# Chunk-selected attention and an ELU MLP on one core: relu written to SBUF, longer rows for the first loads, a new instruction order

## The chip, the cores and the metric

The kernel runs on one core of one Trainium2 chip. The metric is device time in microseconds. The engines are PE (TensorE), DVE (VectorE), ACT (ScalarE), POOL (GpSimd) and SP (SyncE, which here only issues DMAs).

## The reference

Attention of 4 batches, 8 heads, 768 tokens and 64 dimensions per head, in which each query sees 6 of 24 key chunks of 32 tokens, followed by an MLP over 3072 tokens.

```python
k_min, k_max = min and max of k over each chunk of 32 keys
ub = sum over d of max(q * k_min, q * k_max)        # causal, per query and chunk
top_chunks = the 6 chunks of largest ub
scores = q @ k.T / 8, masked to those chunks and to earlier keys
x = softmax(scores) @ v                             # to (3072, 512)
h = x @ w_in                                        # (3072, 2048)
g = where(h > 0, h, exp(min(h, 0)) - 1)
out = g @ w_out                                     # (3072, 512), float32
```

## The kernel before

The work is cut into pairs of heads (a unit `u` is a batch's pair; 16 in all) and halves of 384 tokens. For a pair, K and Q are loaded from HBM and turned so that the head dimension lies on partitions; chunk minima and maxima are taken; a matmul gives the bounds `ub`; DVE finds the sixth largest (`quad_sel`, L551) and compares against it (L614, both inputs in SBUF); POOL puts the result into extra rows of Q (L631), where it acts as a mask in the score matmul (L672). ACT takes the exp (L699), POOL cuts the causal diagonal (L718), PE multiplies with V (L731), DVE normalises (L747), PE transposes (L756) and ACT stores `xT` (L759). When a batch's four pairs have their `xT`, the MLP of that batch and half can run (`mlp`, L763).

Batch 0 has its own preparation (`first_prep`, L443). K and Q of a pair and half come as 96 partitions with 4 tokens each, a row of 1 KB per head, into the big tiles `gT`, which the MLP uses later, and into `stage` and `kt`; the function `home` says where. `turn` (L492) transposes them on PE by 8 matmuls of 96 columns with a float32 identity (L498). ACT copies K and Q out (L508, L526, L531), DVE reduces K (L514, L521), and POOL casts Q (L548) and V (L539). The other batches use `pair_prep` (L386), with DVE transposes (L409, L427), reductions (L413) and POOL casts (L548, L440).

In the MLP, a chunk `fc` of 128 hidden units takes four matmuls into a PSUM bank (L781), then the ELU, then, when four chunks are there, down matmuls (L838). The ELU of a chunk has three forms:

- batches 0 to 2, chunk listed in `BOTH`: ACT exp to `e` in SBUF (L791), ACT relu in place in PSUM (L796), DVE `min(e - 1, relu)` from SBUF and PSUM (L799)
- batches 0 to 2, other chunks: ACT exp, DVE `t = max(e - 1, h)` (L820), DVE `min(max(h, 0), t)` (L825), each with one input in PSUM
- batch 3 (`FAST`): ACT exp, DVE L809 and L814, two chunks at a time

A list in `BOTH` has the chunks of one half; each batch has two halves.

The order of instructions is worked out in Python before anything is emitted. Every operation is added to a `Plan` with an engine, an estimated duration, its data, the buffers that it takes and frees, and a rank (`prio`). `Plan.order` (L119) goes through time on these estimates: on each engine, of the operations that could start first, the one of lowest rank goes next. Buffers come from small pools: four single PSUM banks shared by the MLP's chunks, its outputs, the turns and the transposes; two double banks for scores; three each of `e`, `t` and `gT`. Operations marked `port=True`, and all of POOL, are planned so that a marked DVE operation and a POOL operation do not overlap. The engines then run their instructions strictly in that order. DMAs of K, Q, V and the output are issued by SP, two of the first Q loads by ACT, the weights by POOL.

```python
add("DVE", dve(step * HALF), pr,
    lambda e=e, t=t, view=view: nc.vector.scalar_tensor_tensor(
        out=tiles[t][:, 0:step], in0=tiles[e][:, 0:step], scalar=1.0, in1=view(),
        op0=AOT.subtract, op1=AOT.max),
    reads=[(e, 0), bh[0]], writes=[t], alloc=[t], free=[e])
```

Here `view()` is the PSUM bank `bh`; it is freed by the second DVE operation.

Of the kernel before, what the change touches and what calls it, by code (L numbers as in the profile page):

```python
# [10 lines left out]
AOT = mybir.AluOpType  # L11
# [6 lines left out]
S = 768  # L18
# [20 lines left out]
BOTH = {0: (0, 1, 4, 5, 8, 9, 12, 13), 1: (0, 1, 2, 3, 4, 5, 8, 9, 10, 11, 12, 13), 2: (1, 5, 9, 13), 3: ()}  # L39
# [13 lines left out]
RATES = (232.0, 232.0, -1.4, 0.75)  # L53
MERGE = (False, False, False, True)

# [8 lines left out]
class Plan:  # L64
# [53 lines left out]

    def order(self):  # L119
# [77 lines left out]
def kernel(  # L197
# [188 lines left out]
    def pair_prep(u):  # L386
# [52 lines left out]
        add("POOL", 0.13 + 0.00096 * S, pr + 1.0,  # L439
# [3 lines left out]
    def first_prep(u, hf):  # L443
# [18 lines left out]
        def home(i):  # L462


            if i < 12:
                if i % 6 == 0:
                    STAGED[i // 6], = new("gT")
                h = STAGED[i // 6]
                return h, [h] if i % 6 == 0 else [], [h] if i % 6 == 5 else [], lambda: tiles[h][:, i % 6]
            h, = new("stage" if i < 15 else "kt")  # L470
            return h, [h], [h], lambda: tiles[h][:, 0:512]
# [13 lines left out]
        (hk, ak, fk, at_k), (hq, aq, fq, at_q) = home(i0), home(i0 + 1)  # L485
        fetch(0.5, 197.0, RATES[0], pl, load(at_k, kw, nc.sync), [(hk, i0)], alloc=ak)
        fetch(0.5, 197.0, RATES[0], pl + 0.1, load(at_q, qw, nc.scalar if early else nc.sync), [(hq, i0 + 1)],
# [4 lines left out]
        def turn(bb, at):  # L492
            def f():
                p_ = ps(bb, [P, HALF], F32)
                for j in range(4):
                    for hd in range(2):
                        x0 = 256 * hd + 64 * j
                        nc.tensor.matmul(p_[64 * hd:64 * hd + 64, 96 * j:96 * j + 96], lhsT=at()[0:96, x0:x0 + 64],  # L498
                                         rhs=ident_f[0:96, 0:96], start=True, stop=True)
            return f  # L500

        def tok(x):

            return x.rearrange("q (j p) -> q p j", j=4)
        add("PE", TURN, pr, turn(bk, at_k), reads=[(hk, i0), "ident"], writes=[bk[0]], alloc=bk, free=fk)
        for hd in range(2):
            add("ACT", act(HALF), pr,
                lambda hd=hd: nc.scalar.activation(  # L508
                    out=tiles[kb][0:64, hd, a:b].rearrange("q (p j) -> q p j", j=4),
                    in_=tok(ps(bk, None, None)[64 * hd:64 * hd + 64, :]), func=AF.Copy),  # L510
                reads=[bk[0]], writes=[(kb, hf, hd), (bk[0], "turn")], alloc=[] if hf or hd else [kb])
        for x, op in ((0, AOT.min), (1, AOT.max)):
# [3 lines left out]
                    in_=ps(bk, None, None).rearrange("q (j c w) -> q c j w", j=4, w=CHUNK // 4),  # L516
# [9 lines left out]
            lambda: nc.scalar.activation(out=tiles[qt][:, a:b].rearrange("q (p j) -> q p j", j=4),  # L526
# [5 lines left out]
                out=tiles[qa][:, lo - SEL0:b - SEL0].rearrange("q (p j) -> q p j", j=4),  # L532
                in_=tok(ps(bq, None, None))[:, (lo - a) // 4:], func=AF.Relu),
# [4 lines left out]
        add("POOL", 0.13 + 0.00096 * HALF, pr + 1.0,  # L538
# [6 lines left out]
    def cast(pr, w, what, **kw):  # L545
# [3 lines left out]
        add("POOL", 0.13 + 0.00096 * w, pr, f, **kw)  # L549
# [213 lines left out]
    def mlp(b, hf):  # L763
        tail = b == B - 1
        if True:
# [3 lines left out]
            for fc in range(0, NFC, step):  # L769
# [24 lines left out]
                if both:  # L794
                    add("ACT", act(step * HALF), pr,
                        lambda view=view: nc.scalar.activation(out=view(), in_=view(), func=AF.Relu),  # L796
                        reads=[bh[0]], writes=[bh[0]])
                    add("DVE", dve(step * HALF), pr,
                        lambda e=e, view=view, fc=fc, gt=gt: nc.vector.scalar_tensor_tensor(  # L799
                            out=tiles[gt][:, fc:fc + step, :], in0=tiles[e][:, 0:step], scalar=1.0, in1=view(),  # L800
                            op0=AOT.subtract, op1=AOT.min),
                        reads=[(e, 0), bh[0]], writes=[(gt, fc + i) for i in range(step)],
                        alloc=[gt] if fc == 0 else [], free=bh + [e])
                    continue
                t, = new("t")
                fast = FAST[b]
                if fast:
                    add("DVE", 0.32 + 0.00021 * step * HALF, pr,
                        lambda e=e, t=t: nc.vector.tensor_scalar(  # L809
                            out=tiles[t][:, 0:step], in0=tiles[e][:, 0:step], scalar1=1.0, scalar2=1.0,  # L810
                            op0=AOT.min, op1=AOT.subtract),
                        reads=[(e, 0)], writes=[t], alloc=[t], free=[e], port=True)
                    add("DVE", dve(step * HALF), pr,
                        lambda t=t, view=view, fc=fc, gt=gt: nc.vector.tensor_tensor(  # L814
                            out=tiles[gt][:, fc:fc + step, :], in0=tiles[t][:, 0:step], in1=view(), op=AOT.max),
                        reads=[t, bh[0]], writes=[(gt, fc + i) for i in range(step)],
                        alloc=[gt] if fc == 0 else [], free=bh + [t])
                    continue
# [118 lines left out]
```

## Time and profile before

| | |
|---|---|
| runs | 280.21, 280.38, 285.49 us; median 280.38 |
| span of the profiled execution (first to last instruction) | 278.4 us, some 2.0 under the median of the runs |
| time of the profiled execution itself | not given beside its span |
| granted TensorE clock | 1.000 |
| DVE, ACT, POOL busy | 204.2, 201.4, 128.0 us |

In the profile, busy time is the union of an engine's instructions. An instruction's recorded duration overlaps a little with that of the next one on its engine, so distances between starts are shorter than durations. Groups of instructions are shown as line, engine, operation, out<-in, shape and count, then busy us and the mean ns of one, then the engine's idle time before them and what ended it.

### The profile page before, as it was taken

The numbers are of one execution on the slowest core, as the hardware profiler recorded it, in microseconds if no ns is written. First come the engines' busy times: TensorE is split into PE (matmuls) and PEld (weight loads), VectorE is DVE, ScalarE is ACT, GpSimd is POOL, SyncE is SP. The second block draws the span as 40 slices with busy tenths as digits, with TensorE's granted clock in tenths as the row PEclk, the third lists the DMA queues.
The fourth block names the chain that finished last, engine by engine and source line by source line (L and its number), as shares of the span: only waits on it lengthen the run. The fifth ranks groups of instructions, "written<-read, shape, count | busy, mean of one in ns | idle before, by whom it ended". The sixth has DMA issues, their size and how long they took to land.

```text
span 278.4 us, 7242 instructions
## 1 busy us (share of the span) xinstructions
PE 266.7 (96%) x2732; PEld 164.0 (59%) x2732; DVE 204.2 (73%) x546; ACT 201.4 (72%) x381; POOL 128.0 (46%) x235
## 2 busy tenths in 40 slices
PE   7989899989999999999999999999999999999994
PEld 7968566644565556655665656565565556555541
DVE  6876965799999989999989588657856434767610
ACT  2879899946699697999899958685868564544311
POOL 5668863356797797966965625102320201000000
PEclk9999999999999999999999999999999999999999
DMA  7999999988998599999497101101101111101122
GB/s 187 232 211 188 197 203 207 146 131 163 189 171 156 73 143 201 165 163 170 87 164 114 38 2 38 40 0 40 39 4 38 40 39 40 38 0 40 38 75 75
DMA packets 111330, 29.82 MB, mean 107 GB/s; under 512 B 101056, under 2 KB 108224, under 8 KB 111296
## 3 DMA queue, kind: packets, MB, share of 16 engines
q1 hardware_dynamic: 106656, 24.78, 48.4%
q0 software_dynamic: 4224, 4.19, 9.2%
q8 instruction: 21, 0.34, 0.6%
q10 hardware_dynamic: 416, 0.39, 0.5%
q14 instruction: 13, 0.11, 0.1%
HBM read 27.26 MB, written 6.29 MB: 121 GB/s over the span
## 4 chain that ended last, share of the span: by engine, by line
PE 68%; ACT 15%; DVE 6%; DMA 4%; issue 3%; SPq 1%; POOL 0%; ACTq 0%; DVEq 0%
PE psM L838 20%; PE psH L781 15%; PE psS L781 7%; PE psMT L838 7%; PE psS L672 7%; ACT pt L699 7%; PE psO L731 5%; ACT e L791 3%; PE psS L580 3%; DMA gT<-in_v_dram 2%; DMA gT<-in_k_dram 2%; ACT psH L796 1%; ACT xT L759 1%; DVE gT L799 1%; PE psT L756 1%
## 5 line engine op out<-in xcount | busy, mean ns | idle before, releaser
L699 ACT ACTIVATE pt<-psS 128x768 bf16<-128x768 f32 (+1 forms) x120 | 91.5, 799 | 4.1 <-PE psS L672 2.6
L781 PE MATMUL psH<-xT,w_in_sb 128*128 128x384 bf16 x384 | 75.2, 325 | 1.6 <-ACT xT L759 0.9
L838 PE MATMUL psM<-w_out_sb,gT 128*128 128x512 bf16 x288 | 72.5, 379 | 0.4 <-DVE gT L825 0.2
L781 PEld LDWEIGHTS <-w_in_sb 128*128 128x128 bf16 x512 | 47.6, 97 | 34.8 <-issue 4.0
L791 ACT ACTIVATE e<-psH 128x384 f32<-128x384 f32 x96 | 48.3, 519 | 22.4 <-PE psH L781 21.9
L838 PEld LDWEIGHTS <-gT 128*128 128x128 bf16 x384 | 36.2, 98 | 35.0 <-DVE gT L825 0.6
L718 POOL TENSOR_SCALAR_AFFINE_SELECT pt<-pt 128x256 bf16<-128x256 bf16 (+1 forms) x56 | 29.0, 519 | 56.7 <-ACT pt L699 55.7
L672 PE MATMUL psS<-rhs,lhs 88*128 88x384 bf16 (+4 forms) x304 | 51.5, 283 | 1.6 <-ACT pt L699 0.9
L672 PEld LDWEIGHTS <-lhs 88*128 88x128 bf16 x304 | 27.8, 97 | 15.8 <-issue 1.5
L631 POOL COPY rhs<-selt 24x192 bf16<-24x192 bf16 (+2 forms) x56 | 25.5, 456 | 21.9 <-DVE selt L620 18.6
L799 DVE SCALAR_TENSOR_TENSOR gT<-e,psH 128x384 bf16<-128x384 f32 x48 | 25.6, 539 | 13.3 <-ACT psH L796 13.2
L731 PEld LDWEIGHTS <-pt 128*128 128x128 bf16 x672 | 27.8, 98 | 11.3 <-issue 3.8
L548 POOL CAST rhs<-qt 64x768 bf16<-64x768 f32 (+1 forms) x40 | 28.5, 711 | 12.3 <-ACT qt L526 6.1
L820 DVE SCALAR_TENSOR_TENSOR t<-e,psH 128x384 bf16<-128x384 f32 x48 | 25.9, 543 | 9.6 <-ACT e L791 9.2
L731 PE MATMUL psO<-vext,pt 128*128 128x65 bf16 x672 | 30.2, 194 | 1.7 <-DVE gT L799 1.1
L791 ACT ACTIVATE e<-psS 128x768 f32<-128x768 f32 x16 | 13.0, 810 | 19.0 <-PE psS L781 19.0
L825 DVE SCALAR_TENSOR_TENSOR gT<-psH,t 128x384 bf16<-128x384 f32 x48 | 25.9, 543 | 0.8
L796 ACT ACTIVATE psH<-psH 128x384 f32<-128x384 f32 x48 | 25.1, 528 | 0.0
L781 PE MATMUL psS<-xT,w_in_sb 128*128 128x384 bf16 x128 | 23.2, 326 | 0.0
L548 POOL CAST lhs<-kt 64x768 bf16<-64x768 f32 x24 | 19.6, 819 | 6.8 <-DVE kt L409 3.7
L838 PE MATMUL psMT<-w_out_sb,gT 128*128 128x512 bf16 x96 | 22.5, 379 | 0.0
L759 ACT ACTIVATE xT<-psT 128x384 bf16<-128x384 bf16 x32 | 16.5, 515 | 4.5 <-PE psT L756 4.4
(66 smaller groups left out, 293.4 us busy)
## 6 DMA issues: line engine op xcount, KB each, us to landing
out_dram<-osb SPq DMA_DIRECT2D x24, 256.0 KB, 2.0
vd<-in_v_dram SPq DMA_DIRECT2D x12, 384.0 KB, 5.2
stage<-in_k_dram SPq DMA_DIRECT2D x48, 96.0 KB, 3.4
stage<-in_q_dram SPq DMA_DIRECT2D x48, 96.0 KB, 3.6
w_in_sb<-in_moe_w_in_dram POOLq DMA_DIRECT2D x4, 512.0 KB, 11.5
w_out_sb<-in_moe_w_out_dram POOLq DMA_DIRECT2D x4, 512.0 KB, 8.8
gT<-in_v_dram SPq DMA_DIRECT2D x16, 96.0 KB, 4.3
gT<-in_k_dram SPq DMA_DIRECT2D x6, 192.0 KB, 5.5
```

The source lines that it names most:

```text
L548: nc.gpsimd.tensor_copy(out=o, in_=i)
L672: nc.tensor.matmul(p_s[:, hd, pc:pc + w], lhsT=tiles[pt_["kb"]][0:64 + NCH, hd, 128 * kb:128 * kb + 128], rhs=tiles[pt_["qb"]][0:64 + NCH, ...
L699: lambda bs=bs, pt=pt, wtot=wtot, lo=lo, at=at: nc.scalar.activation(out=tiles[pt][:, :, lo:lo + wtot], in_=tiles[bs[0]][:, :, at:at + wto ...
L718: nc.gpsimd.affine_select(out=a, in_=a, compare_op=AOT.is_ge, fill=0.0, base=0, pattern=pat, channel_multiplier=-1)
L731: nc.tensor.matmul(po[:, hd, qi, :], lhsT=tiles[pt][:, hd, off:off + 128], rhs=tiles[pt_["vx"]][:, 6 * hd + kb, :], start=(kb == 0), stop= ...
L781: nc.tensor.matmul(ph, lhsT=w_in_sb[:, kk, f0:f0 + 128], rhs=tiles[XT[4 * b + kk]][:, c0:c0 + HALF], start=(kk == 0), stop=(kk == NKK - 1))
L791: lambda e=e, view=view: nc.scalar.activation(out=tiles[e][:, 0:step], in_=view(), func=AF.Exp),
L796: lambda view=view: nc.scalar.activation(out=view(), in_=view(), func=AF.Relu),
L799: lambda e=e, view=view, fc=fc, gt=gt: nc.vector.scalar_tensor_tensor(out=tiles[gt][:, fc:fc + step, :], in0=tiles[e][:, 0:step], scalar=1 ...
L820: lambda e=e, t=t, view=view: nc.vector.scalar_tensor_tensor(out=tiles[t][:, 0:step], in0=tiles[e][:, 0:step], scalar=1.0, in1=view(), op0 ...
L825: lambda t=t, view=view, fc=fc, gt=gt: nc.vector.scalar_tensor_tensor(out=tiles[gt][:, fc:fc + step, :], in0=view(), scalar=0.0, in1=tiles ...
L838: nc.tensor.matmul(pm, lhsT=tiles[gt][:, fc, 128 * tt:128 * tt + 128], rhs=w_out_sb[:, fc, :], start=(fc == 0), stop=(fc == NFC - 1))
```

## The change

1. **ELU of batches 0 to 2.** The relu goes to a bf16 tile `t` in SBUF: by ACT for chunks in `BOTH`, otherwise by DVE as a max with 0 from PSUM. The last step, `min(e - 1, t)` on DVE, reads `e` and `t`, both in SBUF. The PSUM bank is freed by the relu or the max. `BOTH` of batch 0 goes from 8 to 4 chunks, of batch 1 from 12 to 8; batch 2 keeps 4.
2. **K and Q loads of pairs 0 to 2 of batch 0.** They come as 8 tokens (a 2 KB row per head) on 48 partitions; the two halves share a tile, at partitions 0 to 47 and 64 to 111. `turn` uses 16 matmuls of 48 columns for these. Pair 3 stays at 96 partitions.
3. **Order.** `Plan.shift` adds small amounts to ranks, drawn from 66 fixed seeds, each for a stretch of operations. Some estimates differ (POOL's copies, ACT's K copies, the long loads), and a down product's part depends on the part before it.

```diff
-BOTH = {0: (0, 1, 4, 5, 8, 9, 12, 13), 1: (0, 1, 2, 3, 4, 5, 8, 9, 10, 11, 12, 13), 2: (1, 5, 9, 13), 3: ()}
+BOTH = {0: (0, 4, 8, 12), 1: tuple(range(0, 16, 2)), 2: (1, 5, 9, 13), 3: ()}
...
     def order(self):
         ops = self.ops
+        self.shift(SHIFTS)
...
-        add("POOL", 0.13 + 0.00096 * S, pr + 1.0,
+        add("POOL", 0.13 + 0.00084 * S, pr + 1.0,
...
+        long = u < SPLIT[3]
+        jj = 8 if long else 4
+        np_ = HALF // jj
+        r0 = 64 * hf if long else 0
...
-                eng.dma_start(out=at()[0:96].rearrange("p (h x) -> p h x", h=2),
-                              in_=src[u][:, a:b].rearrange("h (p j) d -> p h (j d)", j=4))
+                eng.dma_start(out=at()[r0:r0 + np_], in_=src[u][:, a:b].rearrange("h (p j) d -> p h (j d)", j=jj))
...
-                for j in range(4):
+                for j in range(jj):
                     for hd in range(2):
-                        x0 = 256 * hd + 64 * j
-                        nc.tensor.matmul(p_[64 * hd:64 * hd + 64, 96 * j:96 * j + 96], lhsT=at()[0:96, x0:x0 + 64],
-                                         rhs=ident_f[0:96, 0:96], start=True, stop=True)
+                        nc.tensor.matmul(p_[64 * hd:64 * hd + 64, np_ * j:np_ * j + np_],
+                                         lhsT=at()[r0:r0 + np_, hd, 64 * j:64 * j + 64],
+                                         rhs=ident_f[r0:r0 + np_, r0:r0 + np_], start=True, stop=True)
...
+                fast = FAST[b]
+                if both or not fast:
+                    r, = new("t")
+                    if both:
+                        add("ACT", act(step * HALF), pr,
+                            lambda view=view, r=r: nc.scalar.activation(out=tiles[r][:, 0:step], in_=view(), func=AF.Relu),
+                            reads=[bh[0]], writes=[r], alloc=[r], free=bh)
+                    else:
+                        add("DVE", dve(step * HALF), pr,
+                            lambda view=view, r=r: nc.vector.tensor_scalar(
+                                out=tiles[r][:, 0:step], in0=view(), scalar1=0.0, scalar2=None, op0=AOT.max),
+                            reads=[bh[0]], writes=[r], alloc=[r], free=bh)
                     add("DVE", dve(step * HALF), pr,
-                        lambda e=e, view=view, fc=fc, gt=gt: nc.vector.scalar_tensor_tensor(
-                            out=tiles[gt][:, fc:fc + step, :], in0=tiles[e][:, 0:step], scalar=1.0, in1=view(),
-                            op0=AOT.subtract, op1=AOT.min),
-                        reads=[(e, 0), bh[0]], writes=[(gt, fc + i) for i in range(step)],
-                        alloc=[gt] if fc == 0 else [], free=bh + [e])
+                        lambda e=e, r=r, fc=fc, gt=gt: nc.vector.scalar_tensor_tensor(
+                            out=tiles[gt][:, fc:fc + step, :], in0=tiles[e][:, 0:step], scalar=1.0,
+                            in1=tiles[r][:, 0:step], op0=AOT.subtract, op1=AOT.min),
+                        reads=[(e, 0), r], writes=[(gt, fc + i) for i in range(step)],
+                        alloc=[gt] if fc == 0 else [], free=[e, r])
                     continue
...
+                        + ([(bm[0], part - 1)] if part else []),
```

`shift` adds, for each seed in turn, a rank offset to a stretch:

```python
a = int(draw() * n)                    # where the stretch begins
w = 1 + int(v * v * v * 80)            # how long it is
m = amp * (draw() - 0.5) * 2           # amp between 0.1 and 2.5
for o in ops[a:a + w]:
    if not one or o.eng == ops[a].eng:
        o.prio += m
```

Nine of ten seeds do this; the tenth part offsets all operations in blocks of 5 to 64 by up to 0.8.

More of the change, by code (lines that the diff above doesn't have):

```diff
@@ L548, in f @@
             nc.gpsimd.tensor_copy(out=o, in_=i)
-        add("POOL", 0.13 + 0.00096 * w, pr, f, **kw)
+        add("POOL", 0.13 + 0.00084 * w, pr, f, **kw)
     def quad_sel(g, hf):
@@ L804, in mlp @@
                     continue
                 t, = new("t")
[L806 to L818, printed above, removed]
@@ L840, in mlp @@
                     add("PE", 4 * 0.2165, pr, down,
-                        reads=[("w_out", part)] + [(gt, fc) for fc in range(4 * part, 4 * part + 4)],
+                        reads=[("w_out", part)] + [(gt, fc) for fc in range(4 * part, 4 * part + 4)]
+                        + ([(bm[0], part - 1)] if part else []),
                         writes=[(bm[0], part)], alloc=bm if part == 0 else [],
```

86 lines of the change are left out of this document (54 added, 32 removed), and 4 rows, old and new, of the table SHIFTS.

## The prediction

> **What bounds the kernel now.** I read the page first: engine shares, slices in time, then the chain of work that ended last.
>
> ```profile
> span 278.4 us, 7242 instructions
> PE 266.7 (96%) x2732; PEld 164.0 (59%) x2732; DVE 204.2 (73%) x546; ACT 201.4 (72%) x381; POOL 128.0 (46%) x235
> ...
> PE   7989899989999999999999999999999999999994
> ...
> DVE  6876965799999989999989588657856434767610
> ACT  2879899946699697999899958685868564544311
> POOL 5668863356797797966965625102320201000000
> ...
> PE 68%; ACT 15%; DVE 6%; DMA 4%; issue 3%; SPq 1%; POOL 0%; ACTq 0%; DVEq 0%
> ```
>
> PE is busy 96% of the span and carries 68% of the chain, but a busy PE can hide short waits, so the stages matter. I asked for busy time by stage (columns: stretch, its length, then busy us of PE, PEld, DVE, ACT and POOL with instruction counts).
>
> ```profile
> 0.00:30.00 30.00, 27.00 (x507) 24.01 (x509) 21.73 (x85) 21.78 (x50) 20.77 (x52) 1.00 1.03 204
> 30.00:60.00 30.00, 27.34 (x299) 16.97 (x294) 22.33 (x59) 26.98 (x52) 16.25 (x29) 1.00 1.18 181
> 60.00:150.00 90.00, 87.77 (x967) 52.35 (x966) 85.54 (x237) 75.77 (x146) 69.97 (x119) 1.00 0.95 153
> 150.00:210.00 60.00, 60.00 (x553) 35.69 (x552) 42.45 (x119) 45.31 (x89) 17.86 (x31) 1.00 0.08 27
> ```
>
> Before 30 us PE has 3.0 us of idle time. From 30 to 60 ACT is nearly full (26.98 of 30) and DVE stands idle 7.7 us, mostly waiting for ACT. From 60 to 150 DVE is the full one: 85.54 of 90, idle 4.5. From 150 on PE never stops and DVE has 17.5 us of 60 free. So the end is set by how early DVE has served batches 0 and 1; after that PE works off a fixed queue. POOL is off the chain (0%), yet busy 86.2 us of the 120 between 30 and 150 (16.25 + 69.97), 72%. That number decides my forecast.
>
> The groups of instructions that the change touches, shapes kept apart:
>
> ```profile
> L825 DVE SCALAR_TENSOR_TENSOR gT<-psH,t 128x384 bf16<-128x384 f32 x48 | 25.9, 543 | 0.8
> L820 DVE SCALAR_TENSOR_TENSOR t<-e,psH 128x384 bf16<-128x384 f32 x48 | 25.9, 543 | 9.6 <-ACT e L791 9.2
> L799 DVE SCALAR_TENSOR_TENSOR gT<-e,psH 128x384 bf16<-128x384 f32 x48 | 25.6, 539 | 13.3 <-ACT psH L796 13.2
> L796 ACT ACTIVATE psH<-psH 128x384 f32<-128x384 f32 x48 | 25.1, 528 | 0.0
> ```
>
> **The change part by part.**
>
> **1. Loads and turns of batch 0.** Six K and six Q loads use 2 KB rows on 48 partitions; their half-pairs are turned by 16 matmuls of 48 columns instead of 8 of 96.
>
> ```profile
> 3.22 5.72 DMA gT<-in_v_dram
> ...
> 9.83 5.59 DMA gT<-in_k_dram
> ...
> 15.46 0.90 PE psH L498 x16
> ...
> 18.99 0.81 PE psMT L498 x16
> ```
>
> The chain runs through a V load and then pair 0's second K half (issued 9.83, landed 15.42). That K is SP's 13th DMA now and the 8th in the new order: ahead of it stand three V issues instead of eight. The K wait may go; PE lost about 0.6 us to it, and what is late next is ACT's copies. I take -1.0, between 0 and -5.6 (the whole second transfer leaves the chain). The turns go the other way. In fine slices of the turn at 18.9 us (the second count is of weight loads under way):
>
> ```profile
> 18.90:18.93 0.03, 0.01 (x2) 0.02 (x2) 1.00 1.60 307
> 18.93:18.96 0.03, 0.03 (x2) 0.03 (x2) 1.00 0.79 188
> 18.96:18.98 0.02, 0.02 (x2) 0.02 (x4) 1.00 1.29 269
> ```
>
> The second pair of weight loads begins about 0.05 us after the first, so a pair of loads occupies about that. A pair of matmul passes of 96 columns takes some 0.08 us (8 pairs, 0.81 us in all), of 48 columns then 0.04: the 0.05 of loading decides. Sixteen pairs make some 0.85 us and a start, against 0.81 now: I take +0.2 each, 2.4 us for twelve turns. Bounds: 0 (time by columns) and 9.7 (each pass as long as now, +0.81 x 12). PE's 3.0 us of idle time before 30 us covers 1.4 of it, leaving +1.0; without that cover it is 2.4. Loads and turns together: 0, from -5.6 to +9.7.
>
> **2. ACT work goes to DVE.** A batch's list of chunks with relu on ACT is used for two halves: 2 x (8+12+4) = 48 relus become 2 x (4+8+4) = 32. Each relu shed takes one DVE instruction more, so DVE's elementwise instructions of batches 0 to 2 go from 144 to 160.
>
> ```profile
> 42.59 1.01 DVE L820 SCALAR_TENSOR_TENSOR t<-e,psH 128x384 bf16<-128x384 f32 x2
> 43.52 1.01 DVE L825 SCALAR_TENSOR_TENSOR gT<-psH,t 128x384 bf16<-128x384 f32 x2
> ...
> 50.02 0.39 ACT psH L796
> ...
> 50.99 0.47 DVE t L820
> ```
>
> Two in 1.01 us with 0.55 for the first: 0.47 each on DVE, and 0.39 on ACT. DVE gains 16 x 0.47 = 7.5 us of work, ACT sheds 6.2. Against it: the new max reads PSUM alone and need not wait for the exp; the PSUM bank comes free before the last DVE instruction; and ACT, which starved DVE of 7.7 us between 30 and 60, has less to do there. Half of the 7.5 belongs to batch 1, and the new order lets part of that run past 150 us, where DVE has 17.5 us free. I take -1.0 for all of this, between -5 (two thirds of the 7.7 come back and the added work is hidden) and +7.5 (nothing hides it).
>
> How long is the new last instruction, with e and the relu both in SBUF? The nearest row with two SBUF inputs is the comparison L614.
>
> ```profile
> 36.70 0.45 DVE L614 TENSOR_TENSOR selv<-ubt,thr 128x288 bf16<-128x288 f32 x1
> ...
> 31.13 0.63 DVE L614 TENSOR_TENSOR selv<-ubt,thr 128x288 bf16<-128x288 f32 x1
> ...
> 30.95 1.18 POOL L548 CAST rhs<-qt 64x384 bf16<-64x384 f32 x2 [0.26 <-ACT qt L526]
> ...
> 94.43 0.70 DVE L614 TENSOR_TENSOR selv<-ubt,thr 128x288 bf16<-128x288 f32 x1
> ...
> 94.19 0.64 POOL L718 TENSOR_SCALAR_AFFINE_SELECT pt<-pt 128x512 bf16<-128x512 bf16 x1 [1.16 <-ACT pt L699]
> ...
> 19.56 0.12 DVE L521 TENSOR_TENSOR km<-kx,km 128x12 f32<-128x12 f32 x1
> ...
> 24.64 0.48 DVE L521 TENSOR_TENSOR km<-kx,km 128x12 f32<-128x12 f32 x1
> ...
> 24.06 1.05 POOL L548 CAST rhs<-qt 64x384 bf16<-64x384 f32 x2
> ...
> L614 DVE TENSOR_TENSOR selv<-ubt,thr x14: 260/448/705, 15.5 to 196.9; 128x144 bf16<-128x144 f32 x6, 128x288 bf16<-128x288 f32 x6, 128x432 bf16<-128x432 f32 x2
> ...
> L521 DVE TENSOR_TENSOR km<-kx,km x8: 121/223/508, 8.2 to 32.1; 128x12 f32<-128x12 f32 x8
> ```
>
> With POOL idle (36.70) it takes 0.45 for 288 elements; the elementwise rows give 0.54 for 384, the same cost per element. So I price the new instruction as the old. The Trainium skill ("VectorE: DVE Perf Modes", section on the errata of SBUF sources) would have a fixed 58 cycles from SBUF against 120 from PSUM at 0.96 GHz; by it 96 instructions would save an estimated 6 us, and the forecast would be 281. These rows do not show it.
>
> **3. A new wait: DVE and POOL exclude each other.** The same rows show it. L614 takes 0.45 alone, 0.63 when a POOL cast is running as it starts, 0.70 behind a POOL select. L521 takes 0.12 alone and 0.48 when a cast that ends at 25.11 runs beside it. Both have two SBUF inputs. The elementwise instructions of before have one input in PSUM, and their means (539 to 543) do not show this. The skill ("SBUF — State Buffer", section "Who interferes with whom") has this as a rule: a VectorE instruction with two SBUF inputs and a GpSimd instruction that reads SBUF take the shared port for a whole instruction, and the later one waits. By that rule, the trace agrees. The new last step reads e and t, both in SBUF: 96 such instructions, where the kernel before has 22 (L614 x14, L521 x8). The selections are planned with that exclusion (`port=True`); the new step is not, so nothing in the new order keeps it away from POOL's casts.
>
> Price: the waits in the three rows are 0.18, 0.25 and 0.36, mean 0.26. Count:
>
> ```profile
> 30.00:150.00 120.00, 29.74 (x59) 1.00 1.01 160
> 150.00:210.00 60.00, 16.10 (x33) 1.00 0.08 27
> ```
>
> These are the exps, one for each chunk (L791): 59 between 30 and 150. POOL is busy there 72% of the time: 59 x 0.72 x 0.26 = 11.0 us for DVE. The 4.5 us that DVE has idle from 60 to 150 takes up 3 of it: +8. Behind the waiting instruction on DVE stand the next max, the selection and PV's normalisation (L747), for which PE's transposes wait. After 150 us POOL is busy 30%: 33 x 0.30 x 0.26 = 2.6 us, covered by DVE's 17.5 idle; without that cover it would add 2.6. Bounds: 0 (the step does not meet the exclusion, or waits only where DVE would idle) and 59 x 0.36 = 21.
>
> **4. The rest of the order.** All engines' instructions stand in another order, by shifted ranks. PE's own work is the same but for the turns, and it stays in sequence. Nothing in a row prices an order: I give it 0, from -4 (most of the 4.5 us idle of DVE between 60 and 150) to +4. The new dependency between parts of a down product is between instructions of one engine and costs nothing.
>
> **Sum.** 278.4 + 0 (part 1) - 1 (part 2) + 8 (part 3) + 0 = 285.4 us of span. The median of the runs, 280.38, is 2.0 above the profiled span, so 287.4 us.
>
> **Rivals.**
> - **No exclusion is felt.** For: the L614 and L521 rows are another operation, and POOL, not DVE, may be the one that waits. Against: their waits. Then 278.4 - 1 + 2.0 = 279.4.
> - **Faster.** No exclusion, and the relief of ACT works: DVE gets back 5 of its 7.7 idle us from 30 to 60, and the loads take 2 off the start. 278.4 - 5 - 2 + 2.0 = 273.4. For: ACT at 26.98 of 30 with DVE starved. Against: 7.5 us more DVE work in the stretch where DVE has 4.5 us free.
> - **The shared resource itself fills.** Between 30 and 150 POOL holds 86.2 us, and 59 new steps 59 x 0.47 = 27.7: 113.9 of 120. Then POOL is late too, its puts of the selection (L631) hold up the scores, and PE waits. This decides once both together fill the stretch. With 7 us more, 294.4.
> - **The loads do not come earlier.** They are then hidden as now; part 1 ends at +1.0 and the time at 288.4, inside the main case.
>
> **How the numbers follow.** The exclusion on DVE (287.4) 0.50, of which a fifth lies within 2% of before; no exclusion felt 0.22; the filled resource 0.15; faster 0.13. Two per cent, about what a measurement of this kernel can tell from no change, is 274.8 to 286.0. Faster 0.13; within 0.22 + 0.11 = 0.33; slower 0.39 + 0.15 = 0.54. The likeliest case's own range is 282 to 293. The range of 8 in 10 reaches down into the faster case and up past the filled resource: 275 to 296.
>
> **What would show it.** The new step on DVE has a mean clearly over 543 ns (by my price near 0.54 + 0.72 x 0.26 = 0.73 from 30 to 150), long ones beside POOL casts, and about 0.54 after 180 us, where POOL is mostly idle. The relu on ACT stays near 0.39. DVE's busy time from 30 to 60 rises over 22.3. The long turns take about 1.0 instead of 0.81. If the step stays at 0.54 throughout, part 3 is wrong and the time is near 279; if it is long and the time is still below 281, then DVE was not what set the end.

## The result and the profile after

The changed kernel takes 305.32 us (304.27 to 306.58) beside 280.94 for the kernel before on the same chip: a ratio of 1.0866, 95% interval 1.0808 to 1.0924, or 24 us more. The prediction of 287.4 had the sign, and its range ended at 296. The profiled execution took 305.91, its span 304.2. All ratios here compare executions in the faster of the two states in which these kernels run; in the slower one the granted clock is lower and the time a few per cent longer.

The page of the changed kernel: span, busy time of the engines, slices in time, the chain that ended last.

```profile
span 304.2 us, 7595 instructions
PE 283.8 (93%) x2924; PEld 179.4 (59%) x2924; DVE 223.8 (74%) x562; ACT 199.2 (65%) x365; POOL 142.5 (47%) x235
...
PE   6999997998998989988999898999999999999994
...
DVE  5543249899879999799999999999406834667610
...
PE 49%; DVE 34%; DMA 6%; issue 4%; POOL 3%; ACT 2%; SPq 1%; DVEq 0%; POOLq 0%; ACTq 0%
```

DVE's share of the chain goes from 6% to 34% and its busy time from 204.2 to 223.8. POOL has the same 235 instructions and is busy 14.5 us longer. DVE's first six slices, some 45 us, are half empty or more (5 to 2 tenths), and PE is full from the second one on. Busy time by stage (stretch, length, then PE, PEld, DVE, ACT, POOL):

```profile
0.00:30.00 30.00, 27.55 (x448) 25.77 (x449) 14.48 (x56) 12.84 (x30) 13.17 (x38) 1.00 1.04 167
30.00:60.00 30.00, 27.36 (x374) 20.59 (x372) 19.12 (x58) 19.99 (x41) 15.69 (x28) 0.94 1.12 177
60.00:150.00 90.00, 83.97 (x928) 51.64 (x928) 84.93 (x218) 72.38 (x132) 65.63 (x100) 1.00 0.79 130
150.00:210.00 60.00, 54.62 (x540) 30.89 (x539) 59.65 (x158) 43.38 (x83) 36.84 (x52) 1.00 0.38 68
```

Two things differ. Up to 30 us DVE, ACT and POOL have done a third less than before or worse (14.48, 12.84 and 13.17 against 21.73, 21.78 and 20.77) though PE is as busy. And from 150 to 210 PE, which then had no gap (60.00), now loses 5.4 us, while DVE is full (59.65 against 42.45). The next lines show the new last ELU step and the POOL work beside it (groups with shapes kept apart: busy us, mean ns, idle time before), then the step by stage (stretch, length, DVE busy and count, clock, DMA share, GB/s):

```profile
L851 DVE SCALAR_TENSOR_TENSOR gT<-e,t 128x384 bf16<-128x384 f32 x96 | 67.1, 713 | 5.4 <-ACT t L843 4.7
```

```profile
L592 POOL CAST rhs<-qt 64x768 bf16<-64x768 f32 x24 | 21.5, 896 | 4.2 <-DVE qt L465 3.4
...
L762 POOL TENSOR_SCALAR_AFFINE_SELECT pt<-pt 128x512 bf16<-128x512 bf16 x28 | 19.2, 686 | 18.3 <-ACT pt L743 17.8
```

```profile
30.00:150.00 120.00, 33.62 (x47) 0.99 0.87 142
150.00:215.00 65.00, 25.68 (x35) 1.00 0.36 66
215.00:300.00 85.00, 7.85 (x14) 1.00 0.10 38
```

POOL's groups of the kernel before:

```profile
L548 POOL CAST rhs<-qt 64x768 bf16<-64x768 f32 x24 | 19.7, 821 | 5.6 <-DVE qt L427 4.7
...
L718 POOL TENSOR_SCALAR_AFFINE_SELECT pt<-pt 128x512 bf16<-128x512 bf16 x28 | 17.7, 633 | 7.5 <-ACT pt L699 7.1
```

The step takes 713 ns on average, about 0.72 each up to 150 us (33.62 / 47), and 0.56 once POOL is nearly idle. POOL's cast takes 896 ns where it took 821, its select 686 where it took 633.

The early loss shows in PE's timeline. The kernel before (start, us, operation, count of passes; each float32 matmul is two):

```profile
4.56 1.55 PE L498 MATMUL psH<-ident_f,gT 96*64 96x96 f32 x16 [0.34 <-POOL vext L322]
...
9.56 0.84 PE L498 MATMUL psH<-ident_f,gT 96*64 96x96 f32 x16
...
30.52 0.65 PE L781 MATMUL psH<-xT,w_in_sb 128*128 128x384 bf16 x3
```

and the changed one:

```profile
5.62 1.94 PE L541 MATMUL psH<-ident_f,gT 48*64 48x48 f32 x32 [1.40 <-DMA gT<-in_k_dram]
...
33.12 1.95 PE L541 MATMUL psH<-ident_f,gT 48*64 48x48 f32 x32
...
40.74 1.14 PE L541 MATMUL psMT<-ident_f,gT 48*64 48x48 f32 x32
...
47.61 2.77 PE L825 MATMUL psH<-xT,w_in_sb 128*128 128x384 bf16 x8
```

PE has two speeds. In the kernel before it changes to the fast one at some 9 us; now a turn takes 1.95 up to 33 us, and 1.14 for the same 32 passes at 40.74. The up product's first matmuls move from 30.5 to 47.6, 17 us. The clock column shows 1.00 for 0 to 30 in both kernels: it says nothing of the speed there.

### The profile page after: what moved, and what is told of

It reads as the page before. It is cut to its first block, busy times and chain, and to the rows that moved or that the text cites. A ratio compares the mean times of both kernels' runs of the same rounds, so it can differ in the third digit from the quotient of the medians.

```text
span 304.2 us, 7595 instructions
## 1 busy us (share of the span) xinstructions
PE 283.8 (93%) x2924; PEld 179.4 (59%) x2924; DVE 223.8 (74%) x562; ACT 199.2 (65%) x365; POOL 142.5 (47%) x235
## 4 chain that ended last, share of the span: by engine, by line
PE 49%; DVE 34%; DMA 6%; issue 4%; POOL 3%; ACT 2%; SPq 1%; DVEq 0%; POOLq 0%; ACTq 0%
PE psM L876 12%; DVE gT L851 12%; PE psS L825 7%; PE psMT L876 7%; PE psS L716 6%; DVE t L847 6%; PE psH L825 5%; PE psH L541 3%; DMA vd<-in_v_dram 3%; PE psO L775 3%; PE psMT L541 3%; DVE kt L447 3%; DVE thr L653 3%; DVE on L791 2%; DVE qt L465 2%
## 5 line engine op out<-in xcount | busy, mean ns | idle before, releaser
L743 ACT ACTIVATE pt<-psS 128x768 bf16<-128x768 f32 (+2 forms) x120 | 89.2, 777 | 13.8 <-PE psS L716 9.1
L851 DVE SCALAR_TENSOR_TENSOR gT<-e,t 128x384 bf16<-128x384 f32 x96 | 67.1, 713 | 5.4 <-ACT t L843 4.7
L716 PE MATMUL psS<-rhs,lhs 88*128 88x384 bf16 (+4 forms) x304 | 54.1, 294 | 1.0 <-POOL rhs L675 0.8
L762 POOL TENSOR_SCALAR_AFFINE_SELECT pt<-pt 128x256 bf16<-128x256 bf16 (+1 forms) x56 | 34.1, 614 | 43.7 <-ACT pt L743 42.5
L675 POOL COPY rhs<-selt 24x192 bf16<-24x192 bf16 (+2 forms) x56 | 29.7, 531 | 33.2 <-DVE selt L664 26.5
L847 DVE TENSOR_SCALAR t<-psH 128x384 bf16<-128x384 f32 x64 | 34.2, 540 | 5.5 <-ACT e L835 5.3
L716 PEld LDWEIGHTS <-lhs 88*128 88x128 bf16 x304 | 29.2, 102 | 14.0 <-issue 1.8
L788 DVE RECIPROCAL rc<-psO 128x6 f32<-128x6 f32 x32 | 5.9, 185 | 22.5 <-PE psO L775 22.4
L592 POOL CAST lhs<-kt 64x768 bf16<-64x768 f32 x24 | 21.1, 879 | 2.4 <-DVE kt L447 1.4
L859 DVE TENSOR_SCALAR t<-e 128x768 bf16<-128x768 f32 x16 | 8.9, 559 | 12.1 <-ACT e L835 12.1
```

The source lines that it names most:

```text
L592: nc.gpsimd.tensor_copy(out=o, in_=i)
L675: eng.tensor_copy(out=dst.rearrange("c h (i two x) -> c h i two x", two=2, x=32)[:, :, :, odd, :], in_=tiles[st][r0:r0 + NCH, c0:c0 + n].r ...
L716: nc.tensor.matmul(p_s[:, hd, pc:pc + w], lhsT=tiles[pt_["kb"]][0:64 + NCH, hd, 128 * kb:128 * kb + 128], rhs=tiles[pt_["qb"]][0:64 + NCH, ...
L743: lambda bs=bs, pt=pt, wtot=wtot, lo=lo, at=at: nc.scalar.activation(out=tiles[pt][:, :, lo:lo + wtot], in_=tiles[bs[0]][:, :, at:at + wto ...
L762: nc.gpsimd.affine_select(out=a, in_=a, compare_op=AOT.is_ge, fill=0.0, base=0, pattern=pat, channel_multiplier=-1)
L847: lambda view=view, r=r: nc.vector.tensor_scalar(out=tiles[r][:, 0:step], in0=view(), scalar1=0.0, scalar2=None, op0=AOT.max),
```

## The experiments

Two theories stood at first: the step with two SBUF inputs and POOL hold each other up (1), and the turns of 48 rows keep PE slow (2). The rival to both was the new order (3). The edits are shown in short form.

**One input, 96 rows, both, and the loads and turns alone.**

one_input, in the changed kernel (the step leaves the relu part out, so the result is another one):

```diff
-  nc.vector.scalar_tensor_tensor(out=gT, in0=e, scalar=1.0, in1=r, op0=subtract, op1=min)
+  nc.vector.tensor_reduce(out=gT, in_=e as (384, 1), axis=X, op=max)
```

> The changed kernel in its own order, with one instruction exchanged: the last ELU step of each chunk (96 of them) reads e alone, 384 elements of one SBUF tile, in place of e and t; the relu part is left out of the gate. Theory 1 (a DVE step with two SBUF inputs and POOL wait for each other, and that is most of the loss): the step's mean falls from 713 ns to near 540 at all times, POOL's selects from 686/543 towards 633/405 and its casts from 896 towards 821; DVE alone gives back 96 x 0.17 = 16 us of busy time, and since PE already lost about 10 us of the 25 before 50 us, the time falls by some 10, to about 295. Theory 2 (the 48-row turns keep PE slow up to 40 us, and that is the larger part): the step gets shorter too, but the first matmul of the up product stays near 47.6 us and the time above 290. If the turns are all of it, the time stays within 3 us of 305.

rows96, in the changed kernel:

```diff
-  jj = 8 if long else 4;  r0 = 64 * hf if long else 0
+  jj = 4;  r0 = 0        # 8 matmuls of 96 columns; the tiles and the order stay
```

> The changed kernel in its own order, but K and Q of the three pairs of batch 0 loaded as 4 tokens a row on 96 partitions again and turned by 8 matmuls of 96 columns. Theory 2 (the 48-row turns keep PE at half speed up to 40 us): a turn takes 1.5 us before some 9 us and 0.81 after, the first matmul of the up product comes near 32 us instead of 47.6, and the time falls by 10 to 16, to 289 to 295. Theory 1 (contention of the new ELU step with POOL is most of it): the start gets earlier, DVE's and POOL's work between 30 and 150 eats most of it, and the time stays above 299. Theory 3 (the new order itself costs): neither the start nor the time moves by more than 3.

rows96_one_input has both edits:

> Both edits at once (96-row loads and turns; the last ELU step reads e alone, the relu part left out of the gate): what is left of the change is the order and relu on DVE for 16 more half chunks. If theories 1 and 2 together are the whole loss, the time is 277 to 283, as before. If the order itself costs, it stays over 286. If the two losses cover each other (DVE late only because PE was late, or the other way round), this run gains clearly more than the two single ones together, or clearly less.

before_rows48, in the kernel before, its order untouched:

```diff
-  home(i) -> tile on 96 partitions, 4 tokens a row
+  home(i) -> for the 12 tiles in gT: 48 partitions from 0 or 64, 8 tokens a row; 16 matmuls of 48 columns
```

> The kernel before, its order unchanged, with K and Q of the three pairs of batch 0 loaded as 8 tokens on 48 partitions and turned by 16 matmuls of 48 columns: part 1 of the change alone. Theory 2: PE runs at half speed far longer than to 9.3 us, a turn takes about 1.7 us there, and the time rises by 8 to 16, to 289 to 297. By my prediction's part 1 (turns +0.2 each, partly hidden, loads gain 1) it stays within 2 us of 281. Theory 1 and 3 also expect no more than 3.

Measured, as ratios to the kernel before:

| | ratio | interval | us more (ratio less 1, times 281) |
|---|---|---|---|
| changed kernel | 1.0866 | 1.0808 to 1.0924 | 24.3 |
| one_input | 1.0340 | 1.0225 to 1.0455 | 9.6 |
| rows96 | 1.0525 | 1.0387 to 1.0663 | 14.8 |
| rows96_one_input | 1.0004 | 0.9959 to 1.0049 | 0.1 |
| before_rows48 | 1.0313 | 1.0216 to 1.0410 | 8.8 |

The two edits give back 14.7 and 9.6, each with 3 to 4 us either way by the intervals, and together all 24: within that, the losses add up and do not cover each other. Loads and turns alone cost the kernel before 8.8, against 9.6 in the changed one. The loads themselves are not what is late: in the changed kernel PE has no idle time from 5.62 to 44 us and waits for no DMA there, while in rows96, with fast turns, it waits 2.71 us for a K load. In rows96 the turns are fast from the second one on and the up product starts 14 us earlier, of which the end sees 9.6:

```profile
5.27 0.84 PE L541 MATMUL psMT<-ident_f,gT 96*64 96x96 f32 x16
...
33.56 2.37 PE L825 MATMUL psH<-xT,w_in_sb 128*128 128x384 bf16 x12
```

In before_rows48 it starts at 42.11, 11.6 later than before:

```profile
29.93 1.95 PE L501 MATMUL psMT<-ident_f,gT 48*64 48x48 f32 x32
...
42.11 0.65 PE L785 MATMUL psH<-xT,w_in_sb 128*128 128x384 bf16 x3
```

**Is it the wait for the relu?** Reading e alone also takes away the wait for the relu. Two kernels part these. before_two_inputs, in the kernel before, order and waits unchanged:

```diff
-  nc.scalar.activation(out=view(), in_=view(), func=Relu)              # 48 of 96 chunks
-  scalar_tensor_tensor(out=gT, in0=e[:, 0], in1=view(), ...)
+  nc.scalar.activation(out=e[:, 1], in_=view(), func=Relu)
+  scalar_tensor_tensor(out=gT, in0=e[:, 0], in1=e[:, 1], ...)
```

> The kernel before with its order and its waits; only ACT's 48 relus of batches 0 to 2 write to SBUF instead of their PSUM bank, so that half of the last ELU steps (48 of 96) have two SBUF inputs. The bank is still held until that step. Theory 1 (that form and POOL hold each other up): the step's mean rises from 0.54 to about 0.65 to 0.72, POOL's casts and selects get longer, and the time rises by about half of the 13 to 14 us that one input gave back: 284 to 289. If those 13 to 14 us came from the wait for the relu, which went away together with the second input, or from the order, the time stays within 1.5 us of before and the step's mean may still rise.

The ratio is 1.0150 (1.0066 to 1.0234): 4.2 us for half the steps, 2.4 us either way, from two executions of this kernel, with nothing else changed. The step takes 739 ns where it took 539, a little over the 650 to 720 expected, and POOL's cast 900 where it took 821; ACT's relu is as long as before (522 and 528):

```profile
L799 DVE SCALAR_TENSOR_TENSOR gT<-e 128x384 bf16<-128x384 f32 x48 | 35.2, 739 | 11.3 <-ACT e L796 11.2
```

So the form costs by itself. rows96_one_stream, in rows96:

```diff
-  relu -> r;  scalar_tensor_tensor(out=gT, in0=e, in1=r, ...)
+  relu -> e[:, 1];  tensor_reduce(out=gT, in_=e elements 1 to 384, ...)   # the last one is of the relu
```

> The changed kernel in its own order with 96-row loads and turns; the relu is written (ACT or DVE as before) into the second half of e's tile, and the last ELU step reads 384 elements of that tile from its second element on, the last one of them out of the relu: one SBUF stream, but it waits for both the exp and the relu as the change does. Most of the relu is left out of the gate. If the mutual hold-up with POOL is all of the 14 us that one input gave back (296.5 to 282.1), this takes 280 to 284. If the wait for the relu has a share in it, as half the steps in two-input form costing 4.2 us (so 8 for all) lets expect, it takes 286 to 291. If it was the wait alone, 295 or more.

The ratio is 1.0063 (1.0028 to 1.0098). With both waits kept and one stream, 13.0 of rows96's 14.8 us are back, some 4 us either way. The step and the stages, then the last stage of rows96 beside them:

```profile
L851 DVE TENSOR_REDUCE gT<-e 128x384 bf16<-128x384 f32 x96 | 49.9, 534 | 5.4 <-ACT e L843 4.8
```

```profile
60.00:150.00 90.00, 89.88 (x1058) 56.38 (x1057) 83.72 (x244) 75.58 (x142) 63.93 (x111) 1.00 0.89 149
150.00:210.00 60.00, 59.83 (x520) 34.44 (x518) 45.38 (x124) 42.40 (x82) 26.18 (x43) 1.00 0.23 52
```

```profile
150.00:210.00 60.00, 54.88 (x486) 31.13 (x490) 54.01 (x138) 39.77 (x75) 33.41 (x46) 1.00 0.23 47
```

PE is full again from 60 us on, and the wait for the relu shows 4.8 us of DVE idle time, as in the changed kernel (4.7), without moving the end. The wait's share is about 1.7 us (1.0063 against 1.0004), which the two intervals do not part from nothing. My expectation from before_two_inputs, 286 to 291, was too high: doubling 4.2 us gives 8.4, below the 13.0, though the intervals of both leave room for the same price.

The trace of rows96_one_stream also limits what a late start says. Its clock by slices of 7 us falls to half in the fourth and fifth, with 96-row turns:

```profile
PEclk9985579999999999999999999999999999999999
```

Its up product starts at 39.78, 9.3 us after that of the kernel before, and yet its span is only 3.4 us longer (281.8 against 278.4). So the start of the up product is not the end's loss one to one; the prices here are those of the edits.

**What keeps PE slow?** Either a turn of 48 columns leaves PE waiting for weight loads (2a), or the gap of 1.4 us ahead of the first turn loses the speed that the warming matmuls gave (2b). after_wide, in the changed kernel:

```diff
-  rhs = ident_f[r0:r0 + 48, r0:r0 + 48]
+  rhs = ident_w[r0:r0 + 48, 0:96]        # the identity and 48 columns of zeros, overwritten by the next matmul
```

> The changed kernel in its own order, 48-row loads and 16 matmuls a turn kept, but each turn matmul but the last two moves 96 columns (the identity's 48 and 48 of zeros, which the next matmul overwrites): more work on PE for the same result. Theory 2a (PE is slow because a 48-column turn keeps PE's array too little at work; a pair of weight loads sets the pace at 0.107 us): PE becomes fast as in the kernel with 96 rows, a turn takes 16 x 0.08 = 1.3 us against 1.7 slow, the first matmul of the up product comes at 34 to 40 us instead of 47.6, and the time falls by 4 to 9, to 296 to 301. If the activity plays no part, the turns go at the slow speed with twice the columns, 16 x 0.16 = 2.6 us each, and the time rises by 8 to 11, to 313 to 316. Theory 2b (the gap of 1.4 us between the warming matmuls and the first turn): rises as well, since the gap stays.

after_warm64 and before_warm64 have `WARM = 64` in place of 28.

> The changed kernel with 64 warming matmuls in place of 28: PE goes on without a gap until K0 has landed (5.5 us) and 1 to 2 us beyond. Theory 2b (the gap after the warming matmuls leaves PE slow): the turns take about 0.9 from the first one on, the first matmul of the up product comes at 34 to 38 us, and the time falls to 291 to 297. Theory 2a (the 48-column turns themselves let PE fall back to the slow speed): the first turns are fast, then a turn takes 1.7 again after some 3 to 10 us, the up product starts at 44 us or later and the time stays above 301.

> The kernel before with 64 warming matmuls in place of 28. There the first four turns go at the slow speed (1.5 us against 0.81), 2.7 us in all. Theory 2b: those turns become fast, the first one starts 1.5 to 3.5 us later than 4.56; the two nearly cancel, and the time is 279 to 283. It cannot tell 2a from 2b by the time alone; the trace tells whether PE stays fast from the first turn on. If something later than 30 us depends on the start alone, the time moves with the first up matmul (31.7 us).

after_wide: 1.1121 (1.1001 to 1.1241), 314.28 us. Moving 96 columns did not get PE fast: ten of the twelve long turns are slow, two at 37 to 40 us are not (1.47 each), and the one at 46.33 is slow again (2.69). So 2a falls in the form in which I had it. PE's timeline of this kernel:

```profile
5.18 2.69 PE L547 MATMUL psH<-ident_w,gT 48*64 48x96 f32 x32 [0.95 <-POOL vext L365]
```

after_warm64: 1.0890 (1.0769 to 1.1012), 307.29 us, no better than the change. Its first turns are fast; after a pause of 2.1 us they are slow and stay so up to some 41 us:

```profile
7.58 1.14 PE L541 MATMUL psH<-ident_f,gT 48*64 48x48 f32 x32
...
11.38 1.13 PE L541 MATMUL psH<-ident_f,gT 48*64 48x48 f32 x30
14.60 0.34 PE L541 MATMUL psH<-ident_f,gT 48*64 48x48 f32 x1 [2.09 <-issue]
...
21.32 1.95 PE L541 MATMUL psH<-ident_f,gT 48*64 48x48 f32 x32
```

So the gap at the start is not what does it (2b falls). Pauses do cost speed, however, with 96 rows too. In rows96 the clock reads 0.84 and 0.82 in the 5 us after 15 and after 20, around a wait of 2.71 us for a K load that ends at 17.55, and the turn at 22.70 takes 0.88 again. In rows96_one_stream it stays at 0.50 from 20 to 35 after a wait of 2.29 us up to 18.17, with 96-row turns of 1.55 us. What decides how long PE then stays slow was not taken apart. before_warm64: 0.9990 (0.9962 to 1.0019), all turns fast, the first 2.3 us later, the end unmoved, as expected.

The turns of after_wide and of the kernel before move the same columns a matmul in the same type; what is left between them is the number of rows. The costs by themselves, rows_alone:

```diff
+  for rows, r0, cols in ((96, 0, 96), (48, 0, 48), (48, 0, 96), (96, 0, 48), (64, 0, 96), (32, 0, 96), (128, 0, 96), ...):
+      240 to 480 matmuls, lhsT = x[r0:r0 + rows, 64 columns], rhs = ident[..., cols], without a pause
+  12 x last ELU step, POOL's cast, POOL's select; alone and beside each other
```

> Not the kernel: two disputed costs by themselves, the reference's computation is left out. First eleven stretches of f32 matmuls, each into two halves of a bank with 64 stationary columns as in a turn, without a pause, each after several us in which PE stands idle: 96 rows and 96 columns moved; 48 and 48; 48 and 96; 96 and 48; 64 and 96; 32 and 96; 128 and 96; 64 warming matmuls and then 48 and 48; the same 48 and 48 on partitions 64 to 111; 48 and 48 with one 128x128 bf16 matmul after every 4 pairs, and after every pair. Theory 2c (how many rows of the array are at work decides whether PE gets fast, not the columns): the stretches with 96 and 128 rows go from a pair in 0.16 us (0.107 with 48 columns) to 0.08 (0.055) within 5 us, those with 48 and 32 rows stay slow to their end (13 to 19 us), and 64 shows on which side it lies; one wide matmul among the pairs may be enough to get fast. Theory 2a (weight loads, not columns, fill the time): 48 and 96 gets fast, 48 and 48 and 96 and 48 do not. If all get fast within 5 us, the slow speed in the kernel comes from short pauses between the turns and not from the turns' shape. Then the last ELU step 12 times alone, POOL's cast and select alone, and both beside each other, with t in SBUF and with t in PSUM: theory 1 expects 0.54 alone, 0.55 with t in PSUM beside POOL, and with both inputs in SBUF one DVE step and one POOL instruction taking turns, so that a pair takes the sum of both, 1.3 to 1.4 us.

```profile
4.32 21.73 PE L70 MATMUL turned<-ident,lhs 96*64 96x96 f32 x480 [4.32 <-DVE lhs L60]
33.87 34.37 PE L70 MATMUL turned<-ident,lhs 48*64 48x48 f32 x640 [7.82 <-DVE lhs L81]
76.09 38.66 PE L70 MATMUL turned<-ident,lhs 48*64 48x96 f32 x480 [7.84 <-DVE lhs L81]
122.64 34.37 PE L70 MATMUL turned<-ident,lhs 96*64 96x48 f32 x640 [7.89 <-DVE lhs L81]
164.86 38.66 PE L70 MATMUL turned<-ident,lhs 64*64 64x96 f32 x480 [7.84 <-DVE lhs L81]
211.41 38.66 PE L70 MATMUL turned<-ident,lhs 32*64 32x96 f32 x480 [7.89 <-DVE lhs L81]
257.96 22.87 PE L70 MATMUL turned<-ident,lhs 128*64 128x96 f32 x480 [7.89 <-DVE lhs L81]
```

Each line is one unbroken stretch. 480 passes of 96 columns take 21.73 and 22.87 us with 96 and 128 rows, and 38.66 with 64, 48 and 32: PE stays slow for all 38 us. With 48 columns it stays slow even on 96 rows (34.37). There the columns do not set the pace (0.0537 us a pass, more than half of the 0.0805 for 96 columns); I take it that the weight load of 64 columns does. Three more stretches of 48 rows and 48 columns were run, and all stay at a granted clock of 0.50: on partitions 64 to 111 (34.37 again), and with one 128x128 bf16 matmul after every four pairs or after every pair. A wide matmul in between, which I had thought might be enough, does not help. So both matter: the rows at work and the share of the time in which columns move. If one multiplies them, 96 x 1 gets fast; 96 x 0.75 (a matmul needs 0.0805 x 2 x 48/96 = 0.08 of the 0.107 us) and 64 x 1 do not. That product is a reading of the seven stretches above, not something the runs prove.

The granted clock of that kernel around the 128-row stretch, and around the one that begins fast after 64 warming matmuls and goes on with 48 rows and columns (PE, PEld, DVE, ACT, POOL, then the clock):

```profile
257.00:262.00 5.00, 4.04 (x50) 4.04 (x52) 0.91 (x3) 0.00 (x0) 0.00 (x0) 0.50 0.00 0
262.00:267.00 5.00, 5.00 (x104) 5.00 (x102) 0.00 (x0) 0.00 (x0) 0.00 (x0) 0.81 0.01 3
267.00:281.00 14.00, 13.84 (x336) 13.64 (x332) 0.12 (x1) 0.00 (x0) 0.00 (x0) 1.00 0.01 4
...
295.00:300.00 5.00, 5.00 (x168) 4.89 (x167) 0.00 (x0) 0.00 (x0) 0.00 (x0) 1.00 0.01 3
300.00:305.00 5.00, 5.00 (x124) 5.00 (x121) 0.00 (x0) 0.00 (x0) 0.00 (x0) 0.64 0.02 3
305.00:310.00 5.00, 5.00 (x100) 5.00 (x98) 0.00 (x0) 0.00 (x0) 0.00 (x0) 0.50 0.01 3
```

Turns of 48 by 48 do not only fail to reach the full clock, they lose it: granted 1.00 at 295 to 300, 0.50 from 305 on, with PE at work all the time. The Trainium skill ("TensorE: Matmul & The Clock Gate", section "What's actually happening") has the full clock after some 3.4 us of sustained activity. The stretches of 96 and 128 rows come near that (128 rows: 0.50 for the first 5 us, 1.00 from 264, 6 us after the start); 38 us of unbroken matmuls on 64 rows do not, so what counts as activity is more than a busy PE.

The second half of rows_alone, twelve steps each on DVE (L91 both inputs in SBUF, L94 one in PSUM): first alone, then beside casts, with PSUM beside casts, beside selects.

```profile
521.23 7.07 DVE L91 SCALAR_TENSOR_TENSOR g<-e,r 128x384 bf16<-128x384 f32 x12
...
540.35 12.57 DVE L91 SCALAR_TENSOR_TENSOR g<-e,r 128x384 bf16<-128x384 f32 x12
...
554.12 7.01 DVE L94 SCALAR_TENSOR_TENSOR g<-e,turned 128x384 bf16<-128x384 f32 x12
...
573.57 10.23 DVE L91 SCALAR_TENSOR_TENSOR g<-e,r 128x384 bf16<-128x384 f32 x12
```

```profile
528.57 10.50 POOL L98 CAST c<-kq 64x768 bf16<-64x768 f32 x12
...
539.60 12.92 POOL L98 CAST c<-kq 64x768 bf16<-64x768 f32 x12
```

With one input in PSUM the two do not feel each other (7.01). With both in SBUF, twelve steps and twelve casts take 12.9 us, where one after the other would be 7.07 + 10.50 = 17.6, and side by side without hold-up 10.5. Beside selects the twelve steps take 10.23. They hold each other up, but not for the whole of an instruction, as the rule in "SBUF — State Buffer" (the Trainium skill, section "Who interferes with whom") would have it: a step beside a cast takes 1.05 us, not 1.46.

**The order and the balance.** rows96_psum writes the relu back to its PSUM bank, so that the step has one SBUF input, in rows96:

```diff
-  relu -> r (SBUF), bank freed;  step from e, r
+  relu -> bank;  step from e, bank; bank freed        # shifts 1 to 64 of 66
```

> The changed kernel with 96-row loads and turns, and the relu written back to its PSUM bank by ACT or DVE, so that the last ELU step has one input in SBUF and one in PSUM, and nothing is left out. The bank is freed by the last step, so the order is another one again (64 of the 66 shifts; with all no order is found). Theory 1: the step takes 0.54 throughout, and the time is near that of the kernel with one input, 279 to 285. If the two-input form costs nothing and it was the order of the changed kernel that cost, the time lies anywhere, and the step's mean says little: then the step falls to 0.54 and the time stays near 296.

rows96_unshifted is rows96 without the call of `shift`; before_both is the kernel before with the change's `BOTH`.

> The changed kernel with 96-row loads and turns, and without the shifts of the ranks: the planner's own order for the new ELU steps. With the shifts it took 296.5. If the shifted order is worth what my prediction said (0, from -4 to +4), this lies between 292 and 301. Theory 3 (the new order costs): it is under 290. If the shifts find an order that suits the new step, it is over 301.

> The kernel before with the change's lists of chunks whose relu ACT does (32 half chunks instead of 48), in before's own forms of the ELU steps: the balance between ACT and DVE alone, with the order that the planner makes of it. My prediction's part 2 gives -1, from -5 to +7.5: 279 to 288. If the balance or the order made anew costs more than that, it is over 288.

rows96_psum: 1.0481 (1.0379 to 1.0583), far from the 279 to 285 that I expected. Its step takes 538 ns, so the hold-up is gone, and yet the time is that of rows96. That is the outcome that I had named for a form that costs nothing. rows96_one_stream, which keeps the order of rows96 and takes 13.0 us less, speaks against that reading. From 60 to 90 us PE works only 26.36 of 30 and DVE 25.06:

```profile
60.00:90.00 30.00, 26.36 (x260) 14.86 (x259) 25.06 (x66) 19.96 (x38) 16.25 (x27) 1.00 0.71 124
```

Nothing is full there. The bank is held longer and the order is another one; which of the two it is was not taken apart, so this run says nothing on the price of the hold-up. rows96_unshifted: 1.0612 (1.0496 to 1.0728), the same as rows96 within the intervals: the shifts are worth nothing measurable. before_both: 1.0194 (1.0108 to 1.0280), 5.4 us, in the upper part of the expected range: sixteen more DVE instructions, in the order that the planner makes of them, cost 5.4 of the 7.5 us that they take. Not all of that need be DVE's work: in its trace PE waits 2.96 us for a K load up to 15.83, and the clock is 0.50 from 15 to 20.

None of these versions is faster than the kernel before; before_warm64 equals it.

## Why the prediction missed

The sum was 7 us more; 24.3 were measured. By its own steps:

- **Part 1, loads and turns, forecast 0.** This step failed: 9.6 us (rows96 against the change; 8.8 alone). The turn was priced from the row at 18.9 us, when PE was already fast. At that speed +0.2 was near: the fast long turns of after_warm64 start (11.38 - 7.58) / 4 = 0.95 apart. But eleven of the twelve long turns ran slow, 1.7 apart where they follow each other (5.62, 7.33, 9.04). The rows at 4.56 and 9.56 (1.55 and 0.84 for the same turn) were in the trace of before, and I did not ask what makes the one into the other. "PE's 3.0 us of idle time covers 1.4" fell with it: PE, without a gap from 5.62 to 44 us, became the limit of that stretch. My upper bound for the turns, +9.7, happens to hold the end's loss, though not by its reason; the forecast's range did not reach to it.
- **Part 2, ACT's work to DVE, forecast -1.** Together with part 4 it measured +1.8 (rows96_one_stream, 1.0063), and that with PE slow from 20 to 35 us. The balance costs the kernel before 5.4, in an order of its own, so in the change something, perhaps the early release of the bank, may give some of that back; that was not tested by itself.
- **Part 3, the hold-up, forecast +8, bounds 0 to 21.** The mechanism was right: 713 ns, 0.72 up to 150 us where I had 0.73, 0.56 late, POOL longer too. The size was off: 13.0 us (rows96 against rows96_one_stream). The term that failed is the one for the steps after 150 us, which I had taken as covered by DVE's 17.5 idle us. There were 35 of them between 150 and 215, at 0.73 (25.68 / 35); DVE was full there (59.65 of 60) and PE waited. The slow turns are not needed for that: rows96 has 31 steps there at 0.71 (22.11 / 31), and its PE idles 5.1 us from 60 to 150 and 5.1 from 150 to 210, against 0.1 and 0.2 in rows96_one_stream. And I priced the wait on DVE alone: POOL was busy 14.5 us longer as well.
- **Part 4, the order, forecast 0.** Right, as far as rows96_unshifted tells.
- **The checks.** The mean of the step and the turn of about 1.0 came as named (the latter only once PE was fast), and ACT's relu got no longer (mean 507 ns, before 528). DVE's busy time from 30 to 60 was to rise over 22.3 and was 19.12, which pointed at the early loss. The rival "the shared resource itself fills" had the right direction with 294.4; rows96, which has the hold-up, the balance and the order, took 296.5. That the resource was full is not shown: in rows_alone steps and casts overlap in part.
- **Two slips that move nothing.** The comparison and the elementwise rows do not cost the same an element (0.45 / 288 is 1.56 ns, 0.54 / 384 is 1.41); the price of 0.54 for the undisturbed step still came near the 0.56 measured. And a fifth of 0.50 is 0.10, not the 0.11 in the chances.

## What to carry to other kernels

Before a turn or any small matmul is split, look at which speed the row runs that its price is taken from, and whether the new shape still gets PE fast: fewer rows or fewer columns can cost nearly twice the time a pass for as long as they dominate (38.66 against 21.73 us here). A DVE step with both inputs in SBUF is dear wherever POOL is busy; an input left in PSUM avoids that, but the bank that it holds may cost as much. A wait priced as covered by idle time must be held against the idle time that the change leaves, not against that of the kernel before.

## What was not expected of the hardware

- 38.66 us of unbroken matmuls on 64 rows and 96 columns at half speed, while 96 rows got fast within the first 5 us (an estimate: 21.73 is 2.4 us over 480 passes at half of the slow 0.0805, so 4.8 us of it were slow).
- The clock column can show 1.00 where PE runs at half speed: the changed kernel from 0 to 30 us. In after_warm64, where the speed had changed once before, the same turns stand under 0.50.

```profile
20.00:30.00 10.00, 10.00 (x167) 9.16 (x168) 4.81 (x23) 5.15 (x13) 4.41 (x10) 0.50 1.11 173
```

- A step and a cast in mutual hold-up take 1.05 to 1.08 us a pair, between the longer one (0.88) and the sum (1.46).
